# Single pieces of a first transform placed between the way back and the second transform

## The chip, the core and the metric

One Trainium2 chip, of which the kernel uses one core. The metric is the device time of one execution in microseconds (us); less is better. Before the change the median of three runs is 1524.33 us (1523.4 to 1526.67).

## What is computed

Four sequences of 11456 tokens with 128 features are multiplied element by element (`x * v`), convolved along the sequence with a filter that a small network makes, and multiplied by `x` again. The result is the input of a mixture of eight experts with one expert per token:

```python
h_filt = (np.maximum(pos_emb @ w1, 0.0) @ w2) * np.exp(-0.01 * pos)[:, None]
Uf = np.fft.rfft(x * v, n=2 * S, axis=1)
Hf = np.fft.rfft(h_filt, n=2 * S, axis=0)
y = np.fft.irfft(Uf * Hf[None], n=2 * S, axis=1)[:, :S]
attn = x * y                      # (4, 11456, 128), the experts' tokens
...
do_compute = tokens @ w_skip > 0  # the others pass unchanged
e_idx = np.argmax(logits, axis=1)
y[mask] = gate_w[mask, None] * (np.maximum(xc[mask] @ w1[e], 0.0) @ w2[e])
out[do_compute] = xc + y
```

The change touches the convolution alone.

## The kernel before

The Fourier transform of length 60 x 64 is written as matmuls. It is cut into four parts `h` of 32 features each (`NP = 4`), and three blocks of the sequence are held side by side. Three stages follow one another.

`first_phase` makes the filter's transform and the first transform (over 60 positions) of part 0. `freq_phase` is the stage of the change. `out_phase` makes the last transform, finds each token's expert, and runs the experts.

**The first transform in steps and pieces.** `First.data` works on one step, which is two pieces. A piece (line 209) is two matmuls of 60 rows by 120 columns by 384, on the two halves of TensorE's rows, into one `ps` accumulator, which ScalarE copies out at line 210. A step first needs its load of `x` and `v` (line 185, SP's queue) and the product of the two (line 192, on GpSimd in this stage). When both pieces of a step are copied, the following step's first piece also issues their store `x1d` (line 197, SP's queue). There are 16 steps to a part.

**The loop of `freq_phase`.** It runs over `n`, 60 groups of four frequencies (15 groups to each of the four parts), and within each over `j`, the two pairs of frequencies of a group. Its program order sets the order on each engine's queue; nothing is reordered later. For each `n` and `j`:

- `mult(n, j)`: VectorE multiplies the transformed signal in the accumulator `xp` with the filter (lines 397, 401, 403, 406); `add` sums the products on GpSimd (lines 412, 413).
- `back(n - 1, j)`, the way back: six matmuls of 64 rows by 128 columns by 384 into a `ps` accumulator (line 426), which ScalarE copies to `z` (line 427).
- `spread(n + 1, j)`, the second transform: four matmuls of 128 rows by 64 columns by 480 into `xp` of this `j` (line 382), then two ScalarE copies `g` and `re` (lines 385, 387). `mult(n + 1, j)` starts after them. There is one `xp` for each `j`, so `spread(n + 1, j)` has to wait until `mult(n, j)` is done.
- after `j = 0` only: `step()` runs pieces of the next part's first transform, and `store()` issues the store of a finished `z` (line 440, SP's queue).

Both `back` and the pieces take their accumulator from one pool of two, in turns: each allocation gets the buffer of the allocation before the last, and waits for its copy.

`step()` spends a credit. Each call adds 28/11 pieces while fewer than 32 pieces are done, and 32/15 after; as long as two pieces' worth is there, two pieces (one step) are run. So a call runs two pieces as a rule, and four in the iterations n = 3, 7, 11, 22 and 37. All 96 pieces are done at n = 40; four run ahead of the loop.

Loads of the second transform's data (`x1`, lines 372 and 373) are issued three groups ahead, first in an iteration, into four buffers.

Of the kernel before, what the change touches and what calls it, by code (L numbers as in the profile page):

```python
# [46 lines left out]
LEAD = 4  # L47
# [3 lines left out]
QX = 4  # L51
# [265 lines left out]
def freq_phase(tc, nc, i, fi, zd, c3, spare, loads):  # L317
# [6 lines left out]
    PER, BD = K1 // KS, B * DH  # L324
# [3 lines left out]
    with (  # L328
# [11 lines left out]
        done = [0]  # L340

        def others():

            fi.mult(fi.STEPS)
            for n in range(fi.STEPS, fi.ALL):
                fi.mult(n + 1)
                fi.ahead(n + 1)
                for _ in fi.data(n, qps):
                    done[0] += 1
                    yield  # L350

        credit = [0.0]

        def step():

            n = fi.STEPS * fi.Q
            credit[0] += (n - LEAD) / (PER - QX) if done[0] < n else n / PER
            while credit[0] >= fi.Q:
                credit[0] -= fi.Q
                for _ in range(fi.Q):  # L360
                    next(todo, None)

        def load(n):
            h, k = divmod(n, PER)
            while done[0] < h * fi.STEPS * fi.Q:
                next(todo)
            ks = slice(KS * k, KS * k + KS)
            if h == 0:
                nc.sync.dma_start(c2(ks.start, KS), i["c2"][k])
            x1 = qx.tile([128, KS, (NS + NB) * DH], F32, name="x1")  # L370
            w = NB * DH
            nc.sync.dma_start(x1[:, :, 0:fi.RUN], fi.x1d[h][ks].rearrange("k c n w -> (c n) k w"))
            nc.sync.dma_start(x1[:, :, fi.RUN:], fi.x1f[ks, :, :, h * w:(h + 1) * w].rearrange("k c n w -> (c n) k w"))
            return x1

        def spread(n, j):

            xp = xps[n, j] = qpx.tile([128, 2, 512], F32, name=f"xp{j}")
            for c in range(2):
                for q in range(2):  # L380
                    k = 2 * q + j
                    nc.tensor.matmul(xp[q * 64:(q + 1) * 64, c, 0:WX + NB * DH], c2(n % PER * KS + k)[:, c * 64:(c + 1) * 64],  # L382
                                     xs[n][:, k], start=True, stop=True)
            g = qp.tile([128, 2, NB, DH], F32, name=f"g{j}")
            nc.scalar.copy(g.rearrange("p c s d -> p c (s d)"), xp[:, :, WX:WX + NB * DH])
            re = qp.tile([128, WX], F32, name=f"re{j}")
            nc.scalar.copy(re, xp[:, 0, 0:WX])  # L387
            gs[n, j] = g, re

        def mult(n, j):  # L390

            xp, (g, re) = xps.pop((n, j)), gs.pop((n, j))
            rows = lambda v: v.rearrange("p (r d) -> p r d", d=DH)
            made = [qp.tile([128, 3, (NB - s) * BD], F32, name=f"y{j}{s}", bufs=3 if s == 0 else 2) for s in range(NB)]
            for s, o in enumerate(made):
                m = (NB - s) * B
                nc.vector.tensor_tensor(o[:, 1:].rearrange("p c (r d) -> p c r d", d=DH),  # L397
                                        xp[:, :, 0:m * DH].rearrange("p c (r d) -> p c r d", d=DH),
                                        g[:, :, s, None].broadcast_to([128, 2, m, DH]), ALU.mult)
            g2 = qp.tile([128, NB, DH], F32, name=f"gs{j}")  # L400
            nc.vector.tensor_tensor(g2, xp[:, 1, WX:WX + NB * DH].rearrange("p (s d) -> p s d", d=DH), g[:, 0], ALU.add)
            sm = xp[:, 0, 0:WX]
            nc.vector.tensor_tensor(sm, xp[:, 1, 0:WX], re, ALU.add)  # L403
            for s, o in enumerate(made):
                m = (NB - s) * B
                nc.vector.tensor_tensor(rows(o[:, 0]), rows(sm[:, 0:m * DH]), g2[:, s, None].broadcast_to([128, m, DH]), ALU.mult)  # L406
            return made

        def add(eng, made):

            y, p1, p2 = made
            eng.tensor_tensor(y[:, :, BD:], y[:, :, BD:], p1, ALU.add)  # L412
            eng.tensor_tensor(y[:, :, 2 * BD:], y[:, :, 2 * BD:], p2, ALU.add)  # L413
            return y

        def back(n, j):
            h, k = divmod(n, PER)
            y = ys.pop((n, j))
            if j == 0:
                zs[n] = qp.tile([128, 2, 2, WX], F32, name="z", bufs=4)  # L420
            z = zs[n]
            zps = qps.tile([128, 2, 512], F32, name="ps")[:, :, 0:WX]
            for a in range(3):
                for q in range(2):
                    rows = slice(q * 64, (q + 1) * 64)
                    nc.tensor.matmul(zps[:, q], c3[rows, a], y[rows, a], start=(a == 0), stop=(a == 2))  # L426
            nc.scalar.copy(z[:, :, j], zps)  # L427
            if n == ALL - 1:
                put(nc.scalar, h, k, z, j)
            elif j == 1 and n >= ALL - 5:  # L430
                put(nc.scalar, h, k, z)
            elif j == 1:
                done_z.append((h, k, z))
            if j == 1:
                del zs[n]

        def put(eng, h, k, z, j=None):
            rows = zd[h, 0:N2 * 2 * K1].rearrange("(n k) w -> n k w", k=K1)[:, KS * k:KS * k + KS]
            if j is None:
                eng.dma_start(rows, z.rearrange("n q j w -> n (q j) w"))  # L440
            else:
                eng.dma_start(rows.rearrange("n (q j) w -> n q j w", j=2)[:, :, j], z[:, :, j])

        def store(eng=nc.sync):
            while done_z:
                put(eng, *done_z.pop())

        done_z = []
        todo = others()
# [7 lines left out]
        for n in range(ALL + 1):  # L457
            if n + QX - 1 < ALL:
                xs[n + QX - 1] = load(n + QX - 1)
            if n >= ALL - PER:  # L460
                next(loads, None)
            for j in range(2):
                if n < ALL:
                    made = mult(n, j)
                    ys[n, j] = add(nc.gpsimd if n < ALL - 1 else nc.vector, made)
                if n > 0:
                    back(n - 1, j)
                if n + 1 < ALL:
                    spread(n + 1, j)
                if j == 0:  # L470
                    step()
                    store()
            if n < ALL:
                del xs[n]
# [887 lines left out]
def program(tc, i, out):  # L1362
# [5 lines left out]
    with tc.tile_pool(name="mc", bufs=1) as mc:  # L1368
        wf = mc.tile([128, 2 * E * F], F32, name="wf")
        fi = First(nc, i, x1d, x1f, mc, wf)  # L1370
        spare = wf[:, fi.used:]
        c3 = mc.tile([128, 3, 128], F32, name="c3")
        with tc.manual_schedule():
            first_phase(tc, fi)
            nc.scalar.dma_start(c3, i["c3"])
            nc.scalar.dma_start(zd[:, N2 * 2 * K1:], i["none"])
            later = {}

            def prepare():

                later["ex"] = Experts(tc, i, out, lists, mc, wf)
                yield
                later["consts"] = out_consts(nc, i, mc)
                for e in range(E):
                    if e % 2 == 0:
                        yield
                    later["ex"].weights(e, 0)

                for e in range(E):
                    if e != 1:  # L1390
                        yield
                    later["ex"].weights(e, 1)
            freq_phase(tc, nc, i, fi, zd, c3, spare, prepare())
        out_phase(tc, i, out, zd, later["ex"], later["consts"])
# [55 lines left out]
```

## Time and profile before

| What | Value |
|---|---|
| Median of three runs | 1524.33 us |
| The profiled execution | 1525.32 us |
| Its span, first to last instruction | 1523.4 us |
| Mean granted TensorE clock | 0.984 of full speed |
| TensorE busy | 1433.7 us (94% of the span) |
| VectorE busy | 1083.8 us (71%) |
| GpSimd busy | 998.7 us (66%) |
| ScalarE busy | 722.0 us (47%) |
| `freq_phase` (second transforms of line 382) | 136.6 to 690.6 us |
| Last two pieces (line 209) start | 545.0 us |

The profiled execution is 1.0 us above the median and 1.9 us longer than its span. Engines are named PE (TensorE's matmuls), PEld (its weight loads), DVE (VectorE), ACT (ScalarE), POOL (GpSimd) and SP (the queue that issues most transfers). A busy share is a mean over stages that have different limits, so it is read stage by stage.

### The profile page before, as it was taken

To read this page: it belongs to the slowest core of one execution; us is meant where nothing else is said; L and a number is where in the kernel's file an instruction comes from. 1 tells how busy PE (TensorE), PEld (TensorE's weight loads), DVE (VectorE), ACT (ScalarE), POOL (GpSimd) and SP (SyncE) were. 2 spreads that over 40 slices of the span, in tenths; PEclk is the share of its full clock that TensorE was granted. 3 is DMA by queue.
4 is the path that set the end of the run, shared out by engine and by line. 5 is a ranking of instruction groups with operands and counts; after the bars stand their busy time and mean duration, and the time that the engine had idled before them with its cause. 6 is when DMAs were issued, how large, how long until landed. Compare 5 with 4: busy or idle time off the path is not lost. (4 is left out here: it accounts for less than half of the span.)

```text
span 1523.4 us, 27014 instructions
## 1 busy us (share of the span) xinstructions
PE 1433.7 (94%) x8624; PEld 887.6 (58%) x8624; DVE 1083.8 (71%) x2688; ACT 722.0 (47%) x1201; POOL 998.7 (66%) x946
## 2 busy tenths in 40 slices
PE   7994999999999999997779999999999999999997
PEld 3551343443444443443457776676778888888887
DVE  1323677777777789996887787787857777777774
ACT  4552444444444443332345554445445555555554
POOL 1111877777777767771265868857786888888765
PEclk9996999999999999999999999999999999999999
DMA  8999999998999888977998889888321111111100
GB/s 310 327 336 333 376 390 374 379 381 306 359 388 349 300 283 296 365 234 276 375 313 268 271 268 310 276 263 271 95 40 38 46 46 45 46 46 45 37 28 24
DMA packets 198348, 362.13 MB, mean 238 GB/s; under 512 B 63352, under 2 KB 138726, under 8 KB 198170
## 3 DMA queue, kind: packets, MB, share of 16 engines
q1 hardware_dynamic: 180198, 317.16, 60.0%
q0 software_dynamic: 16448, 38.88, 9.1%
q10 hardware_dynamic: 1560, 4.36, 0.7%
q8 instruction: 69, 1.13, 0.3%
q14 instruction: 73, 0.60, 0.1%
HBM read 216.91 MB, written 145.37 MB: 238 GB/s over the span
## 5 line engine op out<-in xcount | busy, mean ns | idle before, releaser
L397 DVE TENSOR_TENSOR y<-xp,g 128x768 f32<-128x768 f32 x360 | 226.5, 685 | 109.1 <-ACT re L387 100.9
L412 POOL TENSOR_TENSOR y<-y,y 128x768 f32<-128x768 f32 x118 | 214.2, 1815 | 110.8 <-DVE y L406 110.8
L426 PE MATMUL ps<-y,c 64*128 64x384 f32 x1440 | 264.2, 499 | 14.8 <-ACT wf L210 13.1
L724 POOL DMA_INDIRECT out<-o,ids x182 | 199.8, 1098 | 96.0 <-DVE o L731 60.2
L426 PEld LDWEIGHTS ps<-y,c 64*128 64x128 f32 x1440 | 134.5, 186 | 156.6 <-issue 65.3
L655 POOL DMA_INDIRECT xt<-out,ids x182 | 190.6, 1047 | 46.2 <-issue 27.0
L840 DVE SCALAR_TENSOR_TENSOR hh<-hp,hh 128x1024 fp32r<-128x1024 f32 x122 | 148.7, 1219 | 88.5 <-ACT hh L839 88.4
L427 ACT COPY z<-ps 128x768 f32<-128x768 f32 x120 | 95.9, 799 | 178.9 <-PE ps L426 178.9
L839 ACT ACTIVATE hh<-hp 128x1024 fp32r<-128x1024 f32 x122 | 126.3, 1036 | 88.3 <-PE hp L720 88.3
L406 DVE TENSOR_TENSOR y<-xp,gs 128x384 f32<-128x384 f32 x360 | 130.4, 418 | 4.1
L628 POOL MEMSET idle<- 128x512 f16 x231 | 126.1, 546 | 0.3
L209 PE MATMUL ps<-wf,c 60*120 60x384 f32 x512 | 105.8, 522 | 19.5 <-DVE wf L192 15.6
L413 POOL TENSOR_TENSOR y<-y,y 128x384 f32<-128x384 f32 x118 | 118.0, 1000 | 9.2
L382 PE MATMUL xp<-x,wf 128*64 128x480 f32 x512 | 119.9, 591 | 3.0 <-DVE y L406 3.0
L210 ACT COPY wf<-ps 120x768 f32<-120x768 f32 x128 | 98.1, 804 | 38.0 <-PE ps L209 14.9
L192 POOL TENSOR_TENSOR wf<-wf 124x768 f32<-124x768 f32 x46 | 83.9, 1823 | 42.1 <-DVE xp L403 31.5
L801 PE MATMUL bank<-wd,h 128*128 128x128 f32 x896 | 109.6, 278 | 0.0
L718 PE MATMUL hp<-hl,ws 128*128 128x512 f32 (+1 forms) x256 | 103.1, 403 | 2.0 <-DVE hh L840 1.2
L801 PEld LDWEIGHTS bank<-wd,h 128*128 128x128 f32 x896 | 103.6, 192 | 2.1 <-issue 1.6
L695 DVE TENSOR_TENSOR ws<-wf,ws 128x1024 fp32r<-128x1024 f32 x82 | 99.8, 1218 | 4.4 <-issue 3.4
L382 PE MATMUL xp<-x,c 128*64 128x480 f32 x448 | 102.5, 579 | 0.0
L1101 PE MATMUL wide<-zt,c 128*64 128x512 f32 x384 | 93.7, 622 | 6.3 <-DMA zt<-zd 5.3
(197 smaller groups left out, 2702.7 us busy)
## 6 DMA issues: line engine op xcount, KB each, us to landing
wf<-xv SPq DMA_DIRECT2D x64, 768.0 KB
x1d<-wf SPq DMA_DIRECT2D x64, 720.0 KB
x<-x1d SPq DMA_DIRECT2D x60, 768.0 KB
zt<-zd SPq DMA_DIRECT2D x60, 768.0 KB
zd<-z SPq DMA_DIRECT2D x55, 768.0 KB
out<-xm SPq DMA_DIRECT2D x96, 258.0 KB
ox<-xo SPq DMA_DIRECT2D x96, 256.0 KB
x1f<-fx POOLq DMA_DIRECT2D x16, 720.0 KB
```

The costliest lines, as they stand in the source:

```text
L382: nc.tensor.matmul(xp[q * 64:(q + 1) * 64, c, 0:WX + NB * DH], c2(n % PER * KS + k)[:, c * 64:(c + 1) * 64], xs[n][:, k], start=True, stop ...
L397: nc.vector.tensor_tensor(o[:, 1:].rearrange("p c (r d) -> p c r d", d=DH), xp[:, :, 0:m * DH].rearrange("p c (r d) -> p c r d", d=DH), g[ ...
L406: nc.vector.tensor_tensor(rows(o[:, 0]), rows(sm[:, 0:m * DH]), g2[:, s, None].broadcast_to([128, m, DH]), ALU.mult)
L412: eng.tensor_tensor(y[:, :, BD:], y[:, :, BD:], p1, ALU.add)
L413: eng.tensor_tensor(y[:, :, 2 * BD:], y[:, :, 2 * BD:], p2, ALU.add)
L426: nc.tensor.matmul(zps[:, q], c3[rows, a], y[rows, a], start=(a == 0), stop=(a == 2))
L628: self.nc.gpsimd.memset(self.idle, 0.0)
L655: ins = nc.gpsimd.indirect_dma_start(out=xt[:, j], out_offset=None, in_=self.rows[0:have], in_offset=bass.IndirectOffsetOnAxis(ap=ids[:, j ...
L724: ins = nc.gpsimd.indirect_dma_start(out=self.rows, out_offset=bass.IndirectOffsetOnAxis(ap=ids[:, j:j + 1], axis=0), in_=o, in_offset=Non ...
L801: nc.tensor.matmul(bank[:, j * D:(j + 1) * D], h[f][:, j * 128:(j + 1) * 128], wd[s][:, f * D:(f + 1) * D], start=(f == 0), stop=(f == F / ...
L839: nc.scalar.activation(h[:, 0], hp, AF.Relu)
L840: nc.vector.scalar_tensor_tensor(h[:, 1], hp, 0.0, h[:, 0].bitcast(F32), ALU.max, ALU.subtract)
```

## The change

`step()` is called for both `j`, between `back` and `spread`, where it stood after `spread` and for `j = 0` alone. A call adds half the credit, and spends it piece by piece and not step by step.

```diff
         def step():
 
             n = fi.STEPS * fi.Q
-            credit[0] += (n - LEAD) / (PER - QX) if done[0] < n else n / PER
-            while credit[0] >= fi.Q:
-                credit[0] -= fi.Q
-                for _ in range(fi.Q):
-                    next(todo, None)
+            credit[0] += ((n - LEAD) / (PER - QX) if done[0] < n else n / PER) / 2
+            while credit[0] >= 1:
+                credit[0] -= 1
+                next(todo, None)
...
                 if n > 0:
                     back(n - 1, j)
+                step()
                 if n + 1 < ALL:
                     spread(n + 1, j)
                 if j == 0:
-                    step()
                     store()
```

`next(todo)` runs one piece with what belongs to it: the first piece of a step also issues the following step's product (line 192) and load (line 185) and the step before's store (line 197). No instruction is added or removed. By the credit a call now runs one piece as a rule and two in ten of the 82 halves: six among n = 1 to 11 and four among n = 16 to 39. The last piece falls on n = 40, j = 1 (before: j = 0). Lines behind the change are one less in the changed kernel: 426 is 425, 382 is 381.

TensorE's queue in the middle of the stage (groups 16 and 17 of the second transform, `x1_1882` and `x1_1960`); `xp0` and `xp1` are the accumulators of j = 0 and 1, `ps_` those of the way back and of the pieces. Before:

```order
L382 MATMUL xp0_2064<-x1_1882,wf_58 64x480 x4
L209 MATMUL ps_2075<-wf_58,c1_59 120x384 x2
L209 MATMUL ps_2080<-wf_58,c1_59 120x384 x2
L426 MATMUL ps_2099<-y10_2007,c3_61 128x384 x6
L382 MATMUL xp1_2107<-x1_1882,wf_58 64x480 x4
L426 MATMUL ps_2134<-y00_2041,c3_61 128x384 x6
L382 MATMUL xp0_2142<-x1_1960,wf_58 64x480 x4
```

The same place in the changed kernel:

```order
L381 MATMUL xp0_2071<-x1_1882,wf_58 64x480 x4
L425 MATMUL ps_2095<-y10_2003,c3_61 128x384 x6
L209 MATMUL ps_2103<-wf_58,c1_59 120x384 x2
L381 MATMUL xp1_2107<-x1_1882,wf_58 64x480 x4
L425 MATMUL ps_2134<-y00_2041,c3_61 128x384 x6
L209 MATMUL ps_2144<-wf_58,c1_59 120x384 x2
L381 MATMUL xp0_2149<-x1_1960,wf_58 64x480 x4
L425 MATMUL ps_2173<-y10_2081,c3_61 128x384 x6
L209 MATMUL ps_2181<-wf_58,c1_59 120x384 x2
L209 MATMUL ps_2187<-wf_58,c1_59 120x384 x2
L381 MATMUL xp1_2192<-x1_1960,wf_58 64x480 x4
```

The two pieces that stood ahead of the way back of j = 1 are apart: one behind each way back. The last rows show one of the ten halves with two pieces.

ScalarE's queue at the same place, with the copies that free those accumulators. Before:

```order
L387 COPY re0_2071<-xp0_2064 128x384
L210 COPY wf_58<-ps_2075 120x768
L210 COPY wf_58<-ps_2080 120x768
L427 COPY z_2055<-ps_2099 128x2x384
L385 COPY g1_2112<-xp1_2107 128x192
```

In the changed kernel:

```order
L386 COPY re0_2078<-xp0_2071 128x384
L426 COPY z_2055<-ps_2095 128x2x384
L210 COPY wf_58<-ps_2103 120x768
L384 COPY g1_2112<-xp1_2107 128x192
L386 COPY re1_2114<-xp1_2107 128x384
```

A piece's copy now stands ahead of the copies `g` and `re` that VectorE's next product waits for.

TensorE's queue at the start of the loop (group 1 is `x1_794`). Before:

```order
L382 MATMUL xp1_833<-x1_790,wf_58 64x480 x4
L382 MATMUL xp0_860<-x1_794,wf_58 64x480 x4
L209 MATMUL ps_871<-wf_58,c1_59 120x384 x2
L209 MATMUL ps_876<-wf_58,c1_59 120x384 x2
L382 MATMUL xp1_894<-x1_794,wf_58 64x480 x4
L426 MATMUL ps_922<-y00_846,c3_61 128x384 x6
```

In the changed kernel:

```order
L381 MATMUL xp1_833<-x1_790,wf_58 64x480 x4
L209 MATMUL ps_862<-wf_58,c1_59 120x384 x2
L381 MATMUL xp0_867<-x1_794,wf_58 64x480 x4
L209 MATMUL ps_890<-wf_58,c1_59 120x384 x2
L381 MATMUL xp1_894<-x1_794,wf_58 64x480 x4
L425 MATMUL ps_922<-y00_846,c3_61 128x384 x6
```

The first piece now stands ahead of group 1's first second transform, where it stood behind it.

## Rows read from the trace of the kernel before

**Rows 1.** The page, part 1: busy us, share of the span, instructions.

```profile
PE 1433.7 (94%) x8624; PEld 887.6 (58%) x8624; DVE 1083.8 (71%) x2688; ACT 722.0 (47%) x1201; POOL 998.7 (66%) x946
```

**Rows 2.** Stretches: us, then PE, PEld, DVE, ACT, POOL busy; clock, DMA share, GB/s.

```profile
190.00:228.00 38.00, 36.28 (x188) 15.26 (x188) 27.46 (x59) 18.03 (x32) 29.93 (x21) 1.00 1.02 389
...
457.00:495.00 38.00, 36.62 (x190) 15.32 (x188) 29.00 (x63) 17.32 (x31) 29.24 (x20) 1.00 0.99 349
...
600.00:705.00 105.00, 99.36 (x516) 40.80 (x512) 98.78 (x223) 39.00 (x76) 66.31 (x48) 0.99 0.84 293
```

**Rows 3.** Waits, 150 to 545 us: who for whom; us in total, times, longest.

```profile
PE ps L426 <- ACT wf L210: 12.7, 38, 0.4
```

**Rows 4.** Timeline, PE, one iteration (start, us; in brackets the idle before).

```profile
399.70 2.21 PE L426 MATMUL ps<-y,c 64*128 64x384 f32 x12 [0.34 <-ACT wf L210]
...
401.84 1.83 PE L382 MATMUL xp<-x,c 128*64 128x480 f32 x8
...
403.60 2.21 PE L426 MATMUL ps<-y,c 64*128 64x384 f32 x12
...
405.74 1.83 PE L382 MATMUL xp<-x,c 128*64 128x480 f32 x8
...
407.50 1.55 PE L209 MATMUL ps<-wf,c 60*120 60x384 f32 x8
...
409.40 2.21 PE L426 MATMUL ps<-y,c 64*128 64x384 f32 x12 [0.35 <-ACT wf L210]
```

**Rows 5.** Timeline of the same iteration on POOL, ACT and DVE.

```profile
405.19 1.83 POOL L192 TENSOR_TENSOR wf<-wf 124x768 f32<-124x768 f32 x1
...
405.86 0.80 ACT L427 COPY z<-ps 128x768 f32<-128x768 f32 x1 [1.39 <-PE ps L426]
...
407.66 0.32 ACT L385 COPY g<-xp 128x192 f32<-128x192 f32 x1 [1.00 <-PE xp L382]
...
408.39 1.89 DVE L397 TENSOR_TENSOR y<-xp,g 128x768 f32<-128x768 f32 x3
408.45 1.50 ACT L210 COPY wf<-ps 120x768 f32<-120x768 f32 x2
...
411.08 1.09 DVE L406 TENSOR_TENSOR y<-xp,gs 128x384 f32<-128x384 f32 x3
```

**Rows 6.** Timeline, PE, an iteration with four pieces: its first piece, the way back after.

```profile
217.94 1.55 PE L209 MATMUL ps<-wf,c 60*120 60x384 f32 x8
...
221.64 2.21 PE L426 MATMUL ps<-y,c 64*128 64x384 f32 x12 [0.24 <-ACT wf L210]
```

**Rows 7.** Timeline, PE, first phase: a single piece ahead of a 128-row matmul.

```profile
66.58 0.81 PE L209 MATMUL ps<-wf,c 60*120 60x384 f32 x4
67.32 1.27 PE L277 MATMUL fa<-fw,h 128*64 128x128 f32 x16
```

**Rows 8.** Timeline, PE, end of the stage: three ways back in succession.

```profile
691.07 6.08 PE L426 MATMUL ps<-y,c 64*128 64x384 f32 x36
```

**Rows 9.** Timeline at the loop's start, POOL and PE.

```profile
145.84 1.81 POOL L192 TENSOR_TENSOR wf<-wf 124x768 f32<-124x768 f32 x1 [31.51 <-DVE xp L403]
...
143.25 2.94 PE L382 MATMUL xp<-x,wf 128*64 128x480 f32 x8 [3.05 <-DVE y L406]
147.71 2.92 PE L209 MATMUL ps<-wf,c 60*120 60x384 f32 x8 [1.52 <-POOL wf L192]
150.55 3.47 PE L382 MATMUL xp<-x,wf 128*64 128x480 f32 x8
153.95 2.25 PE L426 MATMUL ps<-y,c 64*128 64x384 f32 x12
```

**Rows 10.** Timeline, PE: the first way back in iteration n = 41.

```profile
550.79 2.21 PE L426 MATMUL ps<-y,c 64*128 64x384 f32 x12
```

**Rows 11.** Timeline, SP and PE: group 44's load issued, its first second transform.

```profile
548.35 1.56 SPq L372 DMA_DIRECT2D x<-x1d  x1
...
568.52 1.83 PE L382 MATMUL xp<-x,c 128*64 128x480 f32 x8
```

## The prediction

> **What bounds the kernel now.** I read the page first, then the stretches, the waits, and the timeline of one iteration. The page puts TensorE at 94% of the span [rows 1], which says where to look and not yet what a change is worth. The stretches say it stage by stage [rows 2]. While pieces are run, TensorE is busy 36.3 to 36.6 of 38 us, VectorE 27.5 to 29.0, GpSimd 29.2 to 29.9, ScalarE 17 to 18. After the last piece (600 to 705 us) VectorE is as full as TensorE. So up to the last piece TensorE is the bound, and what it loses is the stage's loss.
>
> The list of waits names one loss on TensorE that repeats [rows 3]: a way back waits 38 times for ScalarE's copy of a piece, 12.7 us in all. The timeline of one iteration shows it [rows 4]. From one way back of j = 1 to the next it is 409.40 - 399.70 = 9.70 us. In it follow second transform (401.84), way back (403.60), second transform (405.74), two pieces (407.50), and then the hole ahead of 409.40. The cause stands in rows 5: the first piece's copy starts at 408.45. Two copies take 1.50, one about 0.80 like the copy of line 427, so the accumulator is free at 409.25, and the way back starts 0.15 later. There are two accumulators and three users in a row: piece, piece, way back. The way back needs the first piece's accumulator.
>
> **What the change removes.** Behind each way back stands one piece, so users alternate: way back, piece, way back, piece. The buffer that a piece wants is that of the previous half's piece, copied by then; the buffer that a way back wants is that of the way back a half earlier. Neither waits. The iteration becomes two equal halves, each way back, piece, second transform. I price a half by start-to-start times, since TensorE's busy times overlap.
>
> Way back to piece: no row shows it. The way back takes 401.84 - 399.70 = 2.14 us before a second transform [rows 4]. Three in succession take 6.08, and one alone 2.21 [rows 4, 8], so one that follows its own kind takes (6.08 - 2.21) / 2 = 1.94. A piece uses TensorE like a way back (two matmuls on the two halves of the rows), so the price lies between 1.94 and 2.14. I take the middle, 2.04, since the pieces have other rows, columns and weights.
>
> Piece to second transform: in the first phase one piece ahead of a 128-row matmul takes 67.32 - 66.58 = 0.74 [rows 7]. The other bound is a third of 1.94 (one of a way back's three pairs of matmuls) and the whole 0.20 that a second transform adds behind a way back: 0.85. I take 0.79, between them.
>
> Second transform to what follows: 1.76, whether a way back or a piece (403.60 - 401.84, 407.50 - 405.74) [rows 4].
>
> A half is 2.04 + 0.79 + 1.76 = 4.59, an iteration 9.18; bounds 4.44 and 4.75, or 8.88 and 9.50.
>
> On the 0.20 the Trainium skill has a rule (TensorEngine Tiling (Array Packing), Key Properties): a change of the tiling mode drains TensorE, a change of the tile within a mode does not. The 2.14 against 1.94 agrees with it. By it a piece behind a way back would drain nothing and pay the whole switch itself, 1.94 + 0.85 + 1.76 = 4.55 a half, which would make the kernel some 2 us faster than my sum. As the order moves two switches and adds none, it gives no result of its own.
>
> Halves with two pieces: their second piece needs the accumulator of the way back just ended. Its copy starts 2.26 after the way back (405.86 - 403.60), takes 0.80, and TensorE restarts 0.15 later [rows 4, 5]: the second piece starts at 3.21, where the first started at 2.04. Each such half costs 3.21 - 2.04 = 1.17 more (1.07 to 1.27 with the bounds above), and there are ten.
>
> **The sum.** Iterations 1 to 40 run from 153.95 to 550.79, 396.8 us [rows 9, 10]. That is 35 x 9.70 and 5 of 11.50 (four pieces take 221.64 - 217.94 = 3.70 [rows 6], two 1.90), 397.0. After: 40 x 9.18 + 10 x 1.17 = 378.9. The gain is 17.9 us, with bounds 28.9 (355.2 + 12.7) and 6.1 (380.0 + 10.7).
>
> **The start takes something back.** The first piece waits for GpSimd's product, which ends at 145.84 + 1.81 = 147.65; TensorE starts it at 147.71 [rows 9]. Before, TensorE made a second transform at 143.25 while it waited; now that stands behind the piece. From 147.71 the old order has pieces and one second transform until 153.95; these rows last nearly twice as long as later ones (3.47 against 1.83). The new order has piece, second transform, piece in that time, and the other second transform behind, at 1.76. So 1.8 us is lost; bounds nothing (the product comes sooner) and 3.5 (it runs slow too). VectorE's first products come later, but their second transforms are due later as well.
>
> **What is moved at no cost, and its cover.** The piece's copy on ScalarE now stands ahead of `g` and `re`. It starts about 0.95 after its piece (408.45 - 407.50) and takes 0.80, so it ends 1.75 after, while the piece and the second transform take 2.55: `g` is not delayed. VectorE starts 408.39 - 405.74 = 2.65 after a second transform starts and is done at 412.17, 6.43 after [rows 4, 5]. The next second transform into that accumulator comes 9.18 after: 2.7 us of cover. VectorE's 3.78 also fit into a half of 4.59. GpSimd has 29.9 of 38 us, and with time a twentieth shorter would have about 31.5 of 38. The product for the next step ends at 407.02 [rows 5] and is used an iteration later. On SP's queue the same transfers are issued; only halves differ. After part 3's last piece, group 44's load, queued behind that piece's store, comes half an iteration later, 4.6 us, of which the cover is the time from issue to use, 568.52 - 548.35 = 20.2 us [rows 11]. From n = 41 on nothing changes, and the later stage starts earlier by what is won: its start is a transfer of this stage's last results.
>
> **The rivals.**
> *Transfers bind in part 0.* In 190 to 228 us transfers are at a share of 1.02 and move 389 GB/s [rows 2]. There the mean iteration falls from (8 x 9.70 + 3 x 11.50) / 11 = 10.19 to (11 x 9.18 + 6 x 1.17) / 11 = 9.82, which asks for 404 GB/s. If 389 is all there is, 11 iterations lose 0.37 each, 4.1 us; the gain is 12.0 and the time 1512. Against it: loads run far ahead, and 4 us can come out of that lead. The Trainium skill (DMA: Bandwidth & Descriptors, Specifications) names a limit of about 358 GB/s from memory to one core. The 389 measured here is above it, so it can't be what decides.
>
> *Every change of shape costs.* Way back to piece at 2.14 and piece to second transform at 0.85, the upper bounds: gain 6.1 - 1.8 = 4.3, time 1520.
>
> *Nothing changes.* The hole moves: TensorE waits 0.2 us in each half for something unnamed. 80 x 0.2 = 16 us, the time stays at 1524. For it: one stall removed often shows the next. Against it: each cover above is over 2 us.
>
> *Slower: the piece blocks the second transform.* A piece whose product is late now holds up the second transform behind it, and so VectorE; before, it stood behind one. Rows 9 show this once. If each of 80 halves waited more than 16.1 / 80 = 0.20 us, the gain would be gone; at 0.5 us the time is 1524 + 24 = 1548. It needs GpSimd's product late by its whole lead, an iteration less the 2 us by which the piece moved forward, or half that where two pieces come together. For it speaks only GpSimd's share.
>
> **How the numbers follow.** The forecast's gain is 17.9 - 1.8 = 16.1. The profiled execution took 1525.32, 1.0 above the median; 1525.32 - 16.1 = 1509.2, and beside the median 1524.33 it is 1508. With the bounds the forecast's own range is 1497 (28.9 - 1.8) to 1522 (6.1 - 3.5). Chances: forecast 0.57, transfers 0.16, every change of shape 0.14, nothing 0.07, slower 0.06. A measurement here tells about 0.2%, 3 us, from no change. The first three are faster: 0.87. For the range I leave out the last two and the low end of the bounds: 1499 to 1520.
>
> **What would show it.** Right: TensorE's wait for line 210 falls from 38 times to about ten, all at halves with two pieces; a half of 4.4 to 4.7 us with way back, piece, second transform; iterations 1 to 40 in about 379 us; at the start one piece at about 147.7 ahead of a second transform. Wrong: second transforms waiting for line 406, ways back for line 413, pieces for line 192, or anything on TensorE for a transfer; or an iteration that stays at 9.7.

## The result, and the profile after

The changed kernel takes 1509.33 us, the median of six runs from 1504.24 to 1515.52, beside 1525.85 for the kernel before in six runs from 1523.4 to 1528.21. The ratio is 0.9896, with a 95% interval of 0.9866 to 0.9926. Set on the 1524.33 that the prediction had, that is about 1508.5; 1508 was forecast. Behind the median, the stage gained 3 us more than the sum had where no load was late, and the start lost 1 less, while late loads, which the sum put at nothing, took 10 us back in the profiled execution. The runs spread over 11 us where those of the kernel before spread over 5; but on the three chips of the later experiments eleven executions of the kernel before spread over 7.5, 9.5 and 12.8 us, so a wide spread is not the change's alone.

The profiled execution after took 1515.03, the second longest of the six. Page, part 1, beside [rows 1]:

```profile
PE 1425.8 (94%) x8624; PEld 888.7 (59%) x8624; DVE 1083.3 (72%) x2688; ACT 718.8 (48%) x1201; POOL 1000.2 (66%) x946
```

The share of TensorE is the same 94%: a page share doesn't show the change. A steady half does. Timeline, PE, to be laid beside [rows 4]:

```profile
396.99 2.21 PE L425 MATMUL ps<-y,c 64*128 64x384 f32 x12
399.03 0.81 PE L209 MATMUL ps<-wf,c 60*120 60x384 f32 x4
399.77 1.83 PE L381 MATMUL xp<-x,c 128*64 128x480 f32 x8
401.54 2.21 PE L425 MATMUL ps<-y,c 64*128 64x384 f32 x12
```

Way back to piece 2.04, piece to second transform 0.74, second transform to the next way back 1.77: a half of 4.55, and no bracket with a wait. A half with two pieces, on PE: the second piece comes 1.16 after the first and waits, as worked out, for the copy of the way back just ended.

```profile
159.51 0.81 PE L209 MATMUL ps<-wf,c 60*120 60x384 f32 x4
160.67 0.91 PE L209 MATMUL ps<-wf,c 60*120 60x384 f32 x4 [0.34 <-ACT z L426]
161.51 1.83 PE L381 MATMUL xp<-x,wf 128*64 128x480 f32 x8
```

The waits from 150 to 535 us show what [rows 3] became, and one wait that wasn't there before (us in total, times, longest):

```profile
POOL wf L192 <- DMA wf<-xv: 22.2, 11, 5.8
...
PE xp L381 <- DMA x<-x1f: 9.0, 5, 2.9
...
PE ps L209 <- ACT z L426: 3.2, 10, 0.3
```

The 38 waits of the way back for a piece's copy are gone. Ten short ones stand at the ten double halves (those with two pieces). The new one is TensorE waiting five times for a load of `x`. Here is one, on PE, and then the place on SP (SyncE's queue) where the load it waits for is issued:

```profile
356.39 0.81 PE L209 MATMUL ps<-wf,c 60*120 60x384 f32 x4
358.94 1.83 PE L381 MATMUL xp<-x,c 128*64 128x480 f32 x8 [1.73 <-DMA x<-x1f]
```

```profile
334.22 0.37 SPq L371 DMA_DIRECT2D x<-x1d  x1
334.64 2.15 SPq L372 DMA_DIRECT2D x<-x1f  x1
336.88 4.49 SPq L439 DMA_DIRECT2D zd<-z  x1
341.47 1.28 SPq L185 DMA_DIRECT2D wf<-xv  x1
342.84 1.19 SPq L197 DMA_DIRECT2D x1d<-wf  x1
344.13 0.37 SPq L371 DMA_DIRECT2D x<-x1d  x1
```

Each turn of SyncE's order is load, store of `z`, next `xv`, store of a product's results, next load. The load issued at 344.13 is needed at 358.94 minus the wait, only 13 us later; the store of `z` ahead of it held the queue for 4.49 us.

So that one execution isn't taken for the kernel, every execution is cut at four marks of TensorE's timeline: the last two of the four pieces that run ahead of the loop (line 209 with a wait for VectorE; the expectations below call them the first phase's last), the first way back, the way back of n = 41, the stage's last way back. For the profile after, beside [rows 9, 10]:

```profile
132.18 2.92 PE L209 MATMUL ps<-wf,c 60*120 60x384 f32 x8 [12.78 <-DVE wf L192]
...
146.15 1.64 PE L209 MATMUL ps<-wf,c 60*120 60x384 f32 x4 [7.23 <-POOL wf L192]
147.72 2.68 PE L381 MATMUL xp<-x,wf 128*64 128x480 f32 x8
...
152.93 2.21 PE L425 MATMUL ps<-y,c 64*128 64x384 f32 x12
...
538.80 2.21 PE L425 MATMUL ps<-y,c 64*128 64x384 f32 x12
```

The same cut for every profiled execution of this study but the one with fewer transfers, which has its numbers below (differences of such rows; "start" is from the first mark to the second, "behind" is the span less the last mark):

| Kernel | first phase to | start | iterations 1 to 40 | 41 to 60 | behind | run, us |
|---|---|---|---|---|---|---|
| before | 133.72 | 20.23 | 396.84 | 147.76 | 824.85 | 1525.32 |
| changed | 132.18 | 20.75 | 385.87 | 147.76 | 826.44 | 1515.03 |
| changed, again | 129.59 | 21.01 | 375.81 | 147.75 | 829.54 | 1505.63 |
| singles behind | 132.50 | 17.24 | 374.87 | 147.65 | 824.34 | 1498.66 |
| pairs between | 133.34 | 20.87 | 400.18 | 147.75 | 829.06 | 1533.21 |
| fifth buffer | 136.94 | 24.57 | 374.84 | 147.75 | 830.10 | 1516.22 |
| z by ScalarE | 132.45 | 23.38 | 377.57 | 147.75 | 827.25 | 1510.35 |
| first piece behind | 134.31 | 17.32 | 376.96 | 147.74 | 831.17 | 1509.45 |
| behind, fifth buffer | 130.30 | 23.54 | 375.23 | 147.64 | 826.29 | 1504.98 |
| fifth buffer late | 132.91 | 21.36 | 376.01 | 147.75 | 837.17 | 1517.34 |
| behind, buffer late | 131.42 | 19.10 | 375.23 | 147.65 | 841.50 | 1516.92 |
| singles behind, again | 132.51 | 18.72 | 374.86 | 147.66 | 840.45 | 1516.02 |

The reader is to see three things. The change's gain stands in the third column, 21 us or 11. What lies behind the stage has the same instructions before and after; it still moves by 7 us between executions in the first nine rows, and stands 6 to 17 us higher in the last three, which ran on another chip. And the start moves from 17 to 25 us, mostly by kernel, but also by 1.5 us between two executions of singles behind.

### The profile page after: what moved, and what is told of

Its sections match the earlier page's. It is cut to its first block, busy times and chain, and to the rows that moved or that the text cites. A ratio compares the mean times of both kernels' runs of the same rounds, so it can differ in the third digit from the quotient of the medians.

```text
span 1513.0 us, 26996 instructions
## 1 busy us (share of the span) xinstructions
PE 1425.8 (94%) x8624; PEld 888.7 (59%) x8624; DVE 1083.3 (72%) x2688; ACT 718.8 (48%) x1201; POOL 1000.2 (66%) x946
## 5 line engine op out<-in xcount | busy, mean ns | idle before, releaser
L425 PEld LDWEIGHTS ps<-y,c 64*128 64x128 f32 x1440 | 129.4, 186 | 152.9 <-issue 53.8
L209 PE MATMUL ps<-wf,c 60*120 60x384 f32 x512 | 109.1, 504 | 25.3 <-DVE wf L192 14.1
L210 ACT COPY wf<-ps 120x768 f32<-120x768 f32 x128 | 102.8, 805 | 39.6 <-issue 23.9
```

## The experiments

**The changed kernel again.** The same program.

> The changed kernel once more, to see how its runs spread. The profile of the first run shows halves of 4.54 us where nothing is late, and about 10 us of waits on TensorE between 320 and 430 us, nearly all for loads of the second transform's data. If late loads are what spreads the runs (1504 to 1516 us), a profile of a run at 1504 to 1506 us has under 2 us of such waits, and one at 1514 or more has about 10. If the spread lies elsewhere (the first or the last stage), the waits are alike in both and iterations 1 to 40 take the same time.

1506.41 us (1502.12 to 1509.97), ratio 0.9888 (0.9866 to 0.991); the kernel before takes 1524.44 on this chip, 18.0 more. All waits of TensorE from 150 to 545 us in its profile:

```profile
PE ps L209 <- ACT z L426: 3.3, 10, 0.3
```

No wait for a load, and iterations 1 to 40 in 375.81 against 385.87: late loads cost the first profile 10 us, and one execution of the program has them and another not. The other is near them: by the ends of packets its loads land as little as 3.2 us ahead of their use, where in the kernel before it is never under 11.7 in these iterations. But the runs spread by 8 us, and this execution is also 2.6 us earlier at the first mark and 3.1 longer behind the stage; the loads are one source of the spread among three at least.

**Singles behind the second transform.** What came of being one by one, what of standing between?

```diff
                 if n > 0:
                     back(n - 1, j)
-                step()
                 if n + 1 < ALL:
                     spread(n + 1, j)
+                step()
```

> Pieces one by one, but behind the second transform and not between it and the way back. If the gain comes of the turns in which two accumulators are used (way back, piece, way back, piece), it stays: the wait of a way back for a piece's copy is gone but for halves with two pieces, a half takes 2.14 + 1.76 + 0.70 = 4.60 us, and the time is 1503 to 1515 us like that of the changed kernel. If the place between the two is what helps, the wait stays and the time is near 1524.

1500.89 us (1498.66 to 1502.45), ratio 0.9854 (0.9832 to 0.9876), faster than the changed kernel on the same chip by 5.5 us between medians, and below the 1503 to 1515 that was expected. All of TensorE's waits from 150 to 545 us, and the start on PE:

```profile
PE ps L425 <- ACT wf L210: 2.7, 10, 0.3
```

```profile
132.50 2.92 PE L209 MATMUL ps<-wf,c 60*120 60x384 f32 x8 [12.52 <-DVE wf L192]
...
143.02 1.83 PE L381 MATMUL xp<-x,wf 128*64 128x480 f32 x8 [3.04 <-issue]
146.40 0.91 PE L209 MATMUL ps<-wf,c 60*120 60x384 f32 x4 [1.55 <-POOL wf L192]
147.24 1.83 PE L381 MATMUL xp<-x,wf 128*64 128x480 f32 x8
149.00 0.91 PE L209 MATMUL ps<-wf,c 60*120 60x384 f32 x4
149.74 2.10 PE L425 MATMUL ps<-y,c 64*128 64x384 f32 x12
154.28 2.10 PE L425 MATMUL ps<-y,c 64*128 64x384 f32 x12
```

The half is 154.28 - 149.74 = 4.54, and iterations 1 to 40 take 374.87, as with the pieces between. So the gain comes from one piece at a time, and not from the place; that it is the alternation of the accumulators is borne out by the waits, but no run here added a third accumulator. The wait is not all of it. Of the 0.62 us that an iteration gains in the changed kernel (9.70 to 9.08), 0.42 is in the two pieces (1.90 with the hole of 0.35 before, twice 0.74 after) and 0.20 in the two ways back (2.14 to 2.04 each). The start differs: TensorE runs the second transform at 143.02 while the product is still made, where the changed kernel stands idle until 146.15. In the runs' own terms it is 17.24 against 20.75 and 21.01.

**Pairs between.** The other half of the change alone: the old `step()` of two pieces for j = 0, put between way back and second transform.

```diff
                 if n > 0:
                     back(n - 1, j)
+                if j == 0:
+                    step()
                 if n + 1 < ALL:
                     spread(n + 1, j)
                 if j == 0:
-                    step()
                     store()
```

> Two pieces together as before, but between the way back and the second transform of j = 0. If the turns of the accumulators matter, the second piece now waits for the way back's own copy: an iteration is 3.21 + 0.79 + 1.76 for j = 0 and 2.14 + 1.76 for j = 1, together 9.66 us, and the time stays at 1523 to 1526. If the place is what helps, the time falls by 10 us or more.

1533.59 us (1531.13 to 1538.93), ratio 1.0073 (1.0046 to 1.01): slower, and by more than was expected. Waits of TensorE from 150 to 560 us, and an iteration with four pieces on PE:

```profile
PE ps L209 <- ACT z L427: 10.1, 40, 0.3
PE ps L209 <- POOL wf L192: 6.7, 5, 1.4
```

```profile
216.35 2.21 PE L426 MATMUL ps<-y,c 64*128 64x384 f32 x12
218.39 0.81 PE L209 MATMUL ps<-wf,c 60*120 60x384 f32 x4
219.46 0.91 PE L209 MATMUL ps<-wf,c 60*120 60x384 f32 x4 [0.25 <-ACT z L427]
221.71 1.55 PE L209 MATMUL ps<-wf,c 60*120 60x384 f32 x8 [1.34 <-POOL wf L192]
```

The wait isn't removed by the place, it moves onto the second piece: 40 times 0.25 us. And where four pieces come together, the third waits 1.34 for GpSimd's product, which with the other four such places makes 6.7 us. Iterations 1 to 40 take 400.18, 3.3 more than before; the start adds 0.6. The 4.2 more behind the stage lie inside what that column does by itself.

**Fewer transfers.** The changed kernel with most filter loads left out.

```diff
+        held = [qx.tile([128, KS, (NS + NB) * DH], F32, name=f"x1{k}", bufs=1) for k in range(QX)]
...
-            x1 = qx.tile([128, KS, (NS + NB) * DH], F32, name="x1")
+            x1 = held[n % QX]
...
-            nc.sync.dma_start(x1[:, :, fi.RUN:], fi.x1f[ks, :, :, h * w:(h + 1) * w].rearrange("k c n w -> (c n) k w"))
+            if n < QX:
+                nc.sync.dma_start(x1[:, :, fi.RUN:], fi.x1f[ks, :, :, h * w:(h + 1) * w].rearrange("k c n w -> (c n) k w"))
```

> The changed kernel, but the filter's part of the second transform's data (192 KB a group in 512 small packets) is loaded for the first four groups only and left in place for the others, so those groups compute with the wrong filter. If the amount of transfers makes loads late, TensorE's waits for loads are gone, iterations 1 to 40 take about 375 us in each run, and the time is 1501 to 1505 with little spread. If the order on SP's queue makes them late (a load stands behind stores that wait for ScalarE's copies), the waits and the spread stay, 1504 to 1515.

Iterations 1 to 40 in 375.8 (152.84 to 528.66) without a wait for a load, as in the repeat that has all its loads. The total, 1559.08, is another program's behind the stage. So with no late load the transfers cost the stage nothing. The waits and the time don't tell whether the number of transfers makes loads late, since the repeat with all of them had no late load either. SyncE's queue does. The stores of z from 150 to 545 us, with the shortest, the middle and the longest issue in ns: before, in the first profile after, and here.

```profile
L440 SPq DMA_DIRECT2D zd<-z x38: 325/342/2845, 163.0 to 530.6; - x38
L439 SPq DMA_DIRECT2D zd<-z x40: 373/1154/9926, 165.8 to 541.8; - x40
L441 SPq DMA_DIRECT2D zd<-z x42: 319/379/2248, 163.8 to 543.4; - x42
```

Together these issues hold SyncE for 18.7, 100.3 and 30.2 us, and for 89.2 in the repeat. The loads of groups 20 to 30 are issued 21.3 to 27.1 us ahead of their use here, 15.8 to 24.7 in the repeat and 11.6 to 18.8 in the first profile after. So in the same order, fewer transfers hold the queue less: their amount has a part in it.

**A fifth buffer for the loads.** Every load one iteration earlier.

```diff
-        tc.tile_pool(name="qx", bufs=QX, reuse_waits="tile") as qx,
+        tc.tile_pool(name="qx", bufs=QX + 1, reuse_waits="tile") as qx,
...
-        xs = {n: load(n) for n in range(QX - 1)}
+        xs = {n: load(n) for n in range(QX)}
...
-            if n + QX - 1 < ALL:
-                xs[n + QX - 1] = load(n + QX - 1)
+            if n + QX < ALL:
+                xs[n + QX] = load(n + QX)
```

> The changed kernel with one more buffer for the x1 loads (5 instead of 4, each load one iteration earlier). Theory A (the loads' lead runs out in some executions, and that is what takes 0 to 10 us of the gain back): the lead grows by about one iteration (9 us), TensorE waits for no load of x between 150 and 545 us, iterations 1 to 40 take 375 to 377 us as in the repeat's profile, median 1501 to 1505, spread of the runs under 5 us. Rival B (the queue is short of bandwidth and a load that starts sooner only ends at the same time): loads still late in some runs, median 1505 to 1510, spread 8 to 11 us. One more load ahead of the loop may cost up to 2 us at the start in either.

1513.25 us (1505.76 to 1516.22), ratio 0.9907 (0.9883 to 0.9932). The median is outside of what theory A gave and the spread is 10 us as rival B had it, though the stage is as A said: 374.84 and no load late. The price lies at the start. GpSimd there, and SP ahead of it:

```profile
152.90 1.80 POOL L192 TENSOR_TENSOR wf<-wf 124x768 f32<-124x768 f32 x1 [32.54 <-DMA wf<-xv]
```

```profile
141.35 0.74 SPq L371 DMA_DIRECT2D x<-x1d  x1
142.13 1.03 SPq L372 DMA_DIRECT2D x<-x1f  x1
143.27 4.01 SPq L185 DMA_DIRECT2D wf<-xv  x3
```

The extra load goes ahead of the three `xv` loads, which are issued from 143.27 on (in the changed kernel from 134.90), and the first product waits for them. The first piece starts at 154.75 instead of 146.15; 4.8 us of that were there at the first mark, and the start takes 24.57. Its runs spread as widely with no late load in the profile.

**Stores of z issued by ScalarE.** The same bytes, but out of SyncE's order.

```diff
-        def store(eng=nc.sync):
+        def store(eng=nc.scalar):
```

> The changed kernel with the z stores issued by ScalarE instead of SyncE: the same bytes, fewer issues in SyncE's order ahead of the loads. Theory A1 (the loads are late because they stand in SyncE's order behind issues that are held up): leads of the loads at iterations 20 to 30 go back to 13 us or more, no wait of TensorE for x, median 1501 to 1505. Rival B (the amount of transfers in parts 1 and 2): leads shrink to 3 to 10 us or 0 as before, median 1505 to 1510. Rival C (an issue held up now holds ScalarE, and the copies that TensorE waits for): waits of TensorE for ScalarE's copies grow from 3 us to 10 or more, median over 1510.

1515.29 us (1510.35 to 1520.05), ratio 0.9941 (0.9923 to 0.996). SP over two loads:

```profile
324.87 0.36 SPq L371 DMA_DIRECT2D x<-x1d  x1
325.30 1.32 SPq L372 DMA_DIRECT2D x<-x1f  x1
329.84 1.06 SPq L185 DMA_DIRECT2D wf<-xv  x1
333.51 0.35 SPq L197 DMA_DIRECT2D x1d<-wf  x1
333.95 0.36 SPq L371 DMA_DIRECT2D x<-x1d  x1
```

The load issued at 324.87 is used at 350.69, 25.8 us later; the same group in the changed kernel was issued at 334.22 and used at 348.05, 13.8 later. By the ends of packets the loads of iterations 20 to 30 now land 13 to 16 us ahead of their use; in the first profile after it was 0.5 to 2.6, in the repeat 3 to 11. That is theory A1: the place of z's stores in SyncE's order makes loads late. It isn't the place alone, since fewer transfers in the same order freed the queue as well: the loads of groups 20 to 30 are issued 21.3 to 27.1 us ahead of their use in both. The time didn't follow. In the profile, which is the fastest of the six runs, the start is 2.4 us longer than in the repeat and iterations 1 to 40 1.8, of which 1.7 is one wait of a way back for GpSimd's sum (line 411). TensorE's waits for copies didn't grow there, so rival C is not shown. Why the other runs are slower is open.

**The first piece alone behind.** Is the start the 5.5 us?

```diff
-                step()
+                if n + j:
+                    step()
                 if n + 1 < ALL:
                     spread(n + 1, j)
+                if n + j == 0:
+                    step()
```

> The changed kernel with the very first piece alone put behind the first second transform (as in the experiment with all pieces behind), every other piece between as changed. If the 5.5 us between the changed kernel and the one with all pieces behind are the start (first phase's last piece to first way back: 21.0 us in the repeat, 17.2 us with all behind, 20.2 us before), the start falls to 17 to 18 us and the median by 3 to 4 us to 1502 to 1505. If they are in the stage (the copy that follows the piece, or the loads), the start falls in the profile and the median stays within 2 us of 1506 to 1509, since the loads then come later for what is gained.

1503.93 us (1502.46 to 1509.45), ratio 0.9858 (0.9839 to 0.9878). The start falls to 17.32, iterations 1 to 40 take 376.96, and the gain over the kernel before on the same chip is 21.3 us, against 18.0 for the repeat. The place of one piece thus makes up most of what singles behind win; the intervals of the ratios overlap, the starts in the profiles don't. Leaving out those with the extra load ahead of the loop, the start is 17.2 to 19.1 in the four profiles with this piece behind, and 20.4 to 23.4 in the five with it ahead.

**Singles behind, with the fifth buffer.** Both edits above together.

> All pieces one by one behind the second transform, with one more buffer for the x1 loads. If no run of the kernel with pieces behind waits for loads (its least lead was 4.4 us in the profile), it stays at 1499 to 1502. If some of its runs do, median 1496 to 1499 and the spread falls from 4 to 2 us.

1506.99 us (1504.61 to 1517.75), ratio 0.9901 (0.9873 to 0.993): higher than the 0.9854 without the buffer, with intervals that just touch. Its start is 23.54, its stage 375.23. I had put no price on the extra load here, though it stood in the expectation beside it.

**The fifth buffer from iteration 8 on,** so that the start keeps its order, in the changed kernel and with singles behind.

```diff
-            if n + QX - 1 < ALL:
-                xs[n + QX - 1] = load(n + QX - 1)
+            for m in range(n + QX - 1 + (n > 8), min(n + QX + (n >= 8), ALL)):
+                xs[m] = load(m)
```

> The changed kernel with a fifth buffer for the x1 loads, the extra load taken in iteration 8, so that the start is as in the changed kernel (first phase's last piece to first way back 20.8 to 21.0 us). Theory A (late loads are one of the things that spread the changed kernel's runs, beside the start and the stages before and after): leads over 8 us at every load from iteration 9 on, iterations 1 to 40 in 375 to 377 us, median 1503 to 1506 (ratio 0.985 to 0.988), spread 5 to 8 us, the rest of it from the parts outside of the stage. Rival (loads were late in one profile alone and cost the median nothing): stage as in A, median 1506 to 1509 (ratio 0.988 to 0.990) as without the buffer.

> All pieces one by one behind the second transform, with the fifth buffer taken in iteration 8. Start 17 to 18 us (with the extra load ahead of the loop it was 23.5), iterations 1 to 40 in 375 us, no late load: 1498 to 1501, ratio 0.983 to 0.985, if loads cost some of its runs anything; equal to the next run within 1.5 us if they cost nothing.

**Singles behind again,** on the same chip as these two.

> All pieces one by one behind the second transform, the same program as before in this study: 1499 to 1503, ratio 0.983 to 0.988, if it is the start that sets it apart from the changed kernel (3 to 4 us); start 17 to 18 us and iterations 1 to 40 in 375 us in the profile. If its first result was luck of the parts outside of the stage, ratio 0.988 to 0.990.

On this chip the kernel before takes 1540.3 us (1531.35 to 1544.16), so only ratios stand. Changed with the late buffer: 1524.5, ratio 0.9909 (0.9881 to 0.9937), start 21.36, stage 376.01, each load from iteration 9 on at least 9 us ahead of its use. Behind with it: 1516.93, 0.9865 (0.9839 to 0.9891). Behind without: 1517.62 (1513.19 to 1535.43), 0.9894 (0.9847 to 0.9941). The buffer does what it should to the leads and shows nothing in the medians: the rival of that expectation is the nearer one, late loads were rare enough to cost the median less than can be measured. The stage of singles behind repeats (374.86), its start is 18.72 and not 17 to 18, and its ratio falls on the side that its expectation called luck: its lead over the changed kernel is not confirmed on this chip, where the part behind the stage is 837 to 841 us.

## Why the prediction was right, and where its terms were not

**The wait removed.** Right. Rows 3's 38 waits are gone, and the two experiments with one half of the change each separate its parts: singles in either place lose the wait, pairs in either place keep one. The ten waits that are left are of a second piece for the way back's own copy (line 426), as the working had it; the list of signs named line 210 for them, which was a slip.

**The half.** 4.54 to 4.55 where 4.59 was forecast. Way back to piece is 2.04, the middle I chose; piece to second transform is 0.74, the lower bound from [rows 7], where I took 0.79. A double half takes 5.70 to 5.80 in the repeat where 4.59 + 1.17 = 5.76 was forecast: the second piece starts 3.20 after the way back, as worked out (3.21), and then takes 0.84 to the second transform.

On this half the Trainium skill's rule (TensorEngine Tiling (Array Packing), Key Properties) is that a change of tiling mode drains TensorE and a change of tile within one does not. By it I had 4.55, with nothing extra from way back to piece (1.94) and the whole switch behind the piece (0.85). The sum agrees, the parts don't: 0.10 more than 1.94 is paid ahead of the piece, and behind it 0.74 as in the first phase.

**Iterations 1 to 40.** This term was mis-sized. The sum said 378.9, a gain of 17.9. Without late loads it is 374.8 to 377.6 in the ten profiles of kernels with singles that show none, 375.81 for the changed kernel, a gain of 21.0. The seventy halves with one piece, 4.543 on average in the repeat in place of 4.59, account for 3.3 us of the difference, and the ten double halves give 0.2 back. With late loads it was 385.87, a gain of 11.0.

**The start.** The mechanism is right: a single piece ahead of the first second transform stands waiting for GpSimd's product, and putting that one piece behind shortens the start by 3.7 us (21.01 to 17.32). Against the kernel before it lost 0.5 to 0.8, not 1.8. I took it that piece, second transform, piece would need the 6.24 us that the old order needs from 147.71 to 153.95 [rows 9]. In the profile after they need 151.17 - 146.15 = 5.02, since the rows there are less stretched (2.68 and 0.91 where 3.47 and twice 1.46 stood). What stretches them is TensorE's clock, which I didn't read. Stretches around the first piece, columns as in [rows 2], before, in the first profile after, and in singles behind:

```profile
143.00:154.00 11.00, 9.23 (x26) 2.65 (x26) 7.46 (x17) 2.30 (x4) 8.08 (x5) 0.54 1.04 408
142.00:150.00 8.00, 3.85 (x12) 1.21 (x12) 3.46 (x8) 0.80 (x1) 5.63 (x4) 0.57 1.02 408
139.00:150.00 11.00, 6.41 (x32) 2.16 (x30) 10.65 (x24) 3.01 (x8) 5.38 (x4) 1.00 1.04 408
```

The granted clock is near half of full speed (the lower level, 1.2 GHz) before and after, and full (2.4 GHz) in singles behind. In the profile after TensorE had been idle for 7.23 us ahead of that piece, in singles behind for 1.55. So the 3.7 us aren't all of them the wait: in singles behind again, with a clock of 0.62 from 142 to 151 us, the start is 18.72 and not 17.24, though TensorE was idle no longer there (0.69).

**The cover of the loads.** This is the step that failed. "What is moved at no cost" gave the loads 20.2 us of cover, the time from issue to use in [rows 11]. By the ends of its packets 10.3 of them are the transfer's own, and the 9.9 that are left are no constant: they shrink when SyncE's queue falls behind. I checked the one load behind part 3's last piece and not the turn of the queue that each load stands in. In the first profile after the lead was used up at n = 20 and stayed so to n = 29, for 10 us. With z's stores in another queue, or with the filter's loads left out, the queue keeps up: order and amount make the loads late together. What this cost the median was too little for the late buffer to show.

**Transfers bind.** The rival had the place wrong and the cause in part: the amount of transfers does count, but through SyncE's queue and not as a rate that can't be passed. In part 0 nothing waited: 190 to 228 us moved 393 GB/s at a share of 1.03, as before. In the stretch with late loads the transfers moved less, not more, while the repeat moved 405 GB/s from 343 to 381 us without a late load:

```profile
190.00:228.00 38.00, 37.31 (x197) 15.86 (x198) 28.79 (x63) 18.61 (x34) 30.25 (x22) 1.00 1.03 393
343.00:381.00 38.00, 34.10 (x179) 14.56 (x179) 27.99 (x62) 17.52 (x31) 26.67 (x18) 1.00 0.92 304
```

**Other covers.** VectorE, ScalarE and GpSimd never held a second transform or a way back by more than 0.4 us in all in the first profile after. GpSimd was to have 31.5 of 38 us; from 190 to 228 us it has 30.25.

**The total.** A gain of 16.1 was forecast, 1525.85 - 1509.33 = 16.5 was measured, 18.0 in the repeat. The repeat's profile is 1523.4 - 1503.7 = 19.7 us shorter than that of before: 21.0 in iterations 1 to 40, less 0.8 at the start, and outside of the change 4.1 earlier at the first mark and 4.7 longer behind. The median's closeness to the forecast is partly luck: a stage gain forecast 3 too small and a start loss 1 too large stand against something that the medians lose. Late loads in some runs are one candidate, but the buffer that removed them moved no median; what lies outside of the stage is another, and which it was isn't shown.

What stays open: why SyncE's queue falls behind further in some executions of the changed kernel than in others; and whether singles behind beat the changed kernel by more than the start. Of all kernels run, singles behind had the lowest median and the lowest ratio.

One number of every execution I left unused: its mean granted clock. The span times what is missing to full clock, as a mean of the executions, is 23 to 25 us for the kernel before on three chips, 26 for the changed kernel in both measurements, 23.6 for singles behind and 23.3 for the first piece behind (the two lowest ratios), 26.4 for singles behind with the fifth buffer, and 27.5 to 28 for z by ScalarE, the fifth buffer and pairs between. On the last chip it is 27 to 30 for the three kernels with singles against 24. So part of what the medians lose may be TensorE's clock outside of iterations 1 to 40, where the profiles of kernels with singles show it full. How much of it fell where TensorE is the bound isn't known.

## What to carry to other kernels

Where two buffers serve three users in a row, put the users in alternation before adding buffers (no run here added an accumulator); the place of each in the order hardly matters in the steady state, but look at the first turn apart, where a product is not yet made. Read the cover of a load from its landing to its use and through the whole turn of the queue that issues it, since a stored tile ahead of it can hold the issue. Where rows of one engine last twice as long as elsewhere, look at its clock there. Where runs of one program spread, cut each execution at the same marks before giving the spread one cause.

## What the runs showed of the hardware

The issue of a store can hold SyncE's queue far longer than it takes elsewhere. SP in the first profile after, and ACT's queue where ScalarE issues the same store:

```profile
312.58 9.93 SPq L439 DMA_DIRECT2D zd<-z  x1
```

```profile
316.28 0.33 ACTq L439 DMA_DIRECT2D zd<-z  x1
```

It is 9.93 us against 0.33, in stretches where the transfers' share was near 1. On SyncE's queue too it stays under 2.9 us in the kernel before and with fewer transfers.

At a share of 1.02 to 1.04 the stretches of these runs moved anything from 361 to 405 GB/s, so a full share says little on the rate. The Trainium skill (DMA: Bandwidth & Descriptors, Specifications) gives some 358 GB/s from memory to one core, as half of what two cores share. This kernel runs on one core, and every such stretch, loads and stores together, is above it; no run here loads a second core.
